# One mLSTM and SwiGLU kernel on one core: the second group's k and q as 32x32 tiles turned by VectorE, and a weight piece asked for earlier

## The chip, the cores and the metric

The kernel runs on one core of a Trainium2 chip. Times are microseconds on the device, of whole executions. A profiled execution also gives a trace: TensorE (PE), VectorE (DVE), ScalarE (ACT), GpSimd (POOL), the queue of SyncE (SP), which asks for most transfers, and the DMA engines that carry them out.

## The reference

Four batches, eight heads, 768 tokens, 40 features a head. The first half is an mLSTM cell with a running maximum in the exponents, the second half a SwiGLU block over the tokens that come out of it (d_model 320, d_ff 1536). Cut to what matters:

```python
for t in range(S):
    m_new = np.maximum(f_gate[:, :, t] + m, i_gate[:, :, t])
    f_stab = np.exp(f_gate[:, :, t] + m - m_new)
    i_stab = np.exp(i_gate[:, :, t] - m_new)
    C = f_stab * C + i_stab * outer(v_t, k_t)        # per batch and head
    n = f_stab * n + i_stab * k_t
    h_tilde = C @ q_t
    denom = np.maximum(np.abs(n @ q_t), 1.0)
    y[:, :, t] = sigmoid(o_gate_t) * h_tilde / denom
x = y as (B * S, H * D)
g = x @ w_gate
out = (g * sigmoid(g) * (x @ w_val)) @ w_out
```

The weights of the second half reach the core as 64-bit numbers and are turned into 32-bit ones there.

## The kernel before

**Groups.** The 768 tokens are six groups of 128 tokens, each for all 32 pairs of batch and head. A group passes first through the cell, then through the SwiGLU block: twelve hidden blocks (`hidden(g, m)`, m = 0 to 11, each ten matmuls into two PSUM banks, a silu on ScalarE and a product on VectorE), then the output matmuls. The cell's work on the next group is laid between the hidden blocks of this one, by hand: a dictionary `slots` says which functions run after which block, `after` does so between the output matmuls of group 0. The schedule is manual: each engine runs its instructions in the order in which the program lists them.

**The cell within a group.** Scores need k and q with features on the partitions (`kT`, `qT`), two heads in 128 rows of which each has 64, the rows past 40 being zero. The weights of the values start from running maxima: the maxima's rows go to DRAM (`M_dram`), come back spread over the partitions into `w_sb` (`weights_load`), are subtracted from the inputs on VectorE (`weights_sub`), masked on GpSimd (`weights_mask`) and raised on ScalarE (`weights_exp`).

**Two ways to turn k and q.** For group 1, `load_all` fetches k and q with tokens on partitions, and `turn(P, ...)` has PE transpose them in 64 matmuls against the identity, with copies from PSUM on ScalarE and VectorE (`turn_one`, L291 to L303). For groups 2 to 5, `load_squares` (L309) fetches 32-token by 32-feature tiles in 16 DMAs, eight of 32 features and eight of the remaining 8, into a tile whose rest is zero, and `turn_squares` (L318) turns every 32x32 block into `kT` or `qT` by two VectorE transposes of 128x1024.

**Pieces.** The SwiGLU weights come as ten pieces (`piece_load`). Pieces 0 to 6 hold the gate and value weights, in two DMAs each; the value half goes out from ScalarE's queue for pieces 0 to 4 and from SP's after that. Pieces 7 to 9 hold the output weights. A conversion of one block is a scaling of two words on ScalarE (`scale`), two bit operations on VectorE (`join`) and a sum on GpSimd or VectorE (`rounded`). Piece 2 carries blocks 2 and 3, piece 6 blocks 10 and 11. `ahead` lists which block is converted inside which hidden block: block 10's conversion is inside hidden block 7, block 11's inside 8.

**PSUM.** Hidden blocks take their two banks from a ring of four ("gen"); the cell has another ring of four ("cell").

**Homes.** `k_sb`, `q_sb`, `v_sb`, `o_sb` hold a group's inputs, `w_sb` its weights, `vw_sb` its weighted values, `x_sb` its results before they are transposed. Each serves one group after another.

**Around the change.** In the start, `sig(0)` and `sig(1)` are the sigmoids of o's two halves on ScalarE, followed there by the requests for the value halves of pieces 2 and 3. After hidden block 0 SP asks for group 1's k and q, after block 1 for piece 6, after block 2 for the maxima and v. `turn` runs after blocks 5 and 6, and the subtractions of the maxima after blocks 6 and 7.

Of the kernel before, what the change touches and what calls it, by code (L numbers as in the profile page):

```python
# [14 lines left out]
ALU = mybir.AluOpType  # L15
# [4 lines left out]
SUB = 64  # L20
# [4 lines left out]
def kernel(  # L25
# [18 lines left out]
    nc = tc.nc  # L44
# [12 lines left out]
    NKC = DM // HP  # L57
    UH = BH // 2
    UA = UH // 2
    NH = NFC + 1  # L60
# [12 lines left out]
    def flat(t):  # L73
        return t.rearrange("p c t -> p (c t)")

    def bank(name, tag="cell"):
        return psum.tile([128, 512], F32, name=name, tag=tag)

    def half(i):
        return slice(i * SUB, (i + 1) * SUB)  # L80
# [5 lines left out]
    def heads(P):  # L86
        return slice(P * UH, (P + 1) * UH)

    k_sb = const.tile([128, BH, DP], F32)
    q_sb = const.tile([128, BH, DP], F32)  # L90
    v_sb = const.tile([128, BH, D1], F32)
    o_sb = const.tile([128, BH, D], F32)
    w_sb = const.tile([128, BH, SUB], F32)
    vw_sb = const.tile([128, BH, D1], F32)
    kT = const.tile([128, PP, L], F32)
    qT = const.tile([128, PP, L], F32)
    x_sb = const.tile([128, B, DM + HP], F32)
# [4 lines left out]
    h_sb = const.tile([128, NH, TW], F32)  # L102
# [3 lines left out]
    ident = const.tile([128, 128], F32)  # L106
# [12 lines left out]
    def copy(eng, dst, src):  # L119
        if eng is nc.scalar:  # L120
            nc.scalar.copy(dst, src)
        else:
            eng.tensor_copy(dst, src)
# [16 lines left out]
    def piece_load(p, home=None):  # L140
        kind, m, n = PIECES[p]
        if kind == "gv":
            a, d = NKC, n * 128
            src = [(slice(i * HP, (i + 1) * HP), w[:, m * 128:(m + n) * 128].rearrange("(c p) f -> p c f", p=HP))
                   for i, w in enumerate((moe_w_gate, moe_w_val))]
            queues = (nc.sync, nc.scalar if p < 5 else nc.sync)
        else:
            a, d = n, DM
            src = [(slice(0, 128), moe_w_out[m * 128:(m + n) * 128].rearrange("(a p) d -> p a d", p=128))]
            queues = (nc.sync,)  # L150
        if src[0][1].dtype == F32:
            for r, w in src:
                if kind == "o":
                    nc.sync.dma_start(out=wo_sb[r, m:m + n, :], in_=w)
                else:
                    for x in range(n):
                        nc.sync.dma_start(out=wgv_sb[r, m + x], in_=w[:, :, ts(x, 128)])
            return
        if home is None:
            raw = conv.tile([128, 4 * NKC * 128], U32, name="raw")  # L160
        else:
            raw = home.rearrange("p a t -> p (a t)").bitcast(U32)
        raw = raw[:, 0:2 * a * d]
        for (r, w), queue in zip(src, queues):
            queue.dma_start(out=raw[r].rearrange("p (a d) -> p a d", a=a), in_=w.bitcast(U32))
        words = raw.rearrange("p (a d two) -> p a d two", two=2, a=a)
        raws[p] = (words[:, :, :, 0], words[:, :, :, 1])
        split(p)
# [4 lines left out]
    def split(p):  # L173
        if p in raws:
            lo, hi = raws.pop(p)
            kind, m, n = PIECES[p]
            if kind == "gv":
                for c in range(n):
                    r = slice(c * 128, (c + 1) * 128)
                    blocks[m + c] = (lo[:, :, r], hi[:, :, r], wgv_sb[:, m + c])  # L180
            else:
                for c in range(0, n, 2):
                    blocks[NFC + (m + c) // 2] = (lo[:, c:c + 2], hi[:, c:c + 2], wo_sb[:, m + c:m + c + 2, :])
# [53 lines left out]
    nc.vector.memset(k_sb[:, :, D:], 0.0)  # L237
    nc.gpsimd.memset(q_sb[:, :, D:], 0.0)
    nc.gpsimd.memset(v_sb[:, :, D:], 1.0)
    ident_b = early.tile([128, 128], BF16)  # L240
    nc.vector.tensor_copy(ident_b, ident)
    mask_b = early.tile([128, L], BF16)
# [35 lines left out]
    def late_maxima():  # L278
        nc.vector.tensor_copy(step1[:, 0:1, 0:1], f0[0:BH, end].unsqueeze(1))
        nc.vector.tensor_copy(step1[:, 1:, 0:1], f_sb[:, 0:NL - 1, last])  # L280
        nc.vector.tensor_tensor_scan(flat(M_sb), flat(step1), flat(i_sb), M0[0:BH, end], op0=ALU.add, op1=ALU.max)
# [6 lines left out]
    M_dram = tc.dram_tile([BH, S - L], F32, name="M_dram")  # L288


    def turn_one(P, src, dst, engs):  # L291
        tp = [bank("tp_kq").rearrange("p (a t) -> p a t", t=SUB) for _ in range(2)]
        for a in range(UA):
            h = P * UH + 2 * a
            for i in range(2):
                nc.tensor.transpose(tp[i][:, a, :], src[half(i), h:h + 2, :].rearrange("p h d -> p (h d)"),  # L296
                                    ident[half(i), half(i)])
        for i in range(2):
            copy(engs[i], dst[:, P * UA:(P + 1) * UA, half(i)], tp[i])

    def turn(P, eng_k, eng_q):
        turn_one(P, k_sb, kT, eng_k)
        turn_one(P, q_sb, qT, eng_q)  # L303

    SQ = 32
# [10 lines left out]
    def turn_squares(src, dst):  # L318
        for P in range(2):
            a = slice(P * UA, (P + 1) * UA)  # L320
            nc.vector.transpose(out=dst[:, a].rearrange("p a t -> p (a t)"), in_=src[:, a].rearrange("p a t d -> p (a t d)"))

    q_sq = q_sb.rearrange("p (a x) d -> p a (x d)", x=2).rearrange("p a (t d) -> p a t d", d=SQ)

    QUAD = ((0, 0), (1, 1), (0, 1), (1, 0))
# [105 lines left out]
    def seam(n, P, engs):  # L431
        engs = list(engs)
        dst = xT(n).rearrange("p c (u i s) -> p c u i s", u=B, i=2)
        for cs in (range(0, 4), range(4, NKC)):
# [6 lines left out]
            for i in range(2):  # L441
                copy(engs.pop(0), dst[:, cs[0]:cs[-1] + 1, 2 * P:2 * P + 2, i, :], tp[i])

    def weights_load(n):
        for i in range(2):
            src = M_dram[:, ds((n - 1) * L + i * SUB, SUB)].unsqueeze(0).to_broadcast([SUB, BH, SUB])
            nc.sync.dma_start(out=w_sb[half(i)], in_=src)

    def weights_sub(n, P):
        gb = g_T[:, n, heads(P)].unsqueeze(2).to_broadcast([128, UH, SUB])  # L450
        nc.vector.tensor_tensor(w_sb[:, heads(P)], gb, w_sb[:, heads(P)], op=ALU.subtract)  # L451

    def weights_mask(P):
        for i in range(2):
# [7 lines left out]
    def sig(P):  # L462
        nc.scalar.activation(o_sb[:, heads(P)], o_sb[:, heads(P)], AF.Sigmoid)
# [10 lines left out]
    A, V, G = nc.scalar, nc.vector, nc.gpsimd  # L474
# [24 lines left out]
    def first_values(P):  # L499
        nc.gpsimd.tensor_copy(w_end[:, heads(P)], W0[:, heads(P), end])  # L500
        nc.gpsimd.tensor_tensor(vw_sb[:, heads(P)], v_sb[:, heads(P)], w_end[:, heads(P)].to_broadcast([128, UH, D1]),
                                op=ALU.mult)
# [24 lines left out]
    def first_own(u):  # L527
        first_y[u] = bank("first_y", "gen")[:, 0:H * D1].rearrange("p (h d) -> p h d", d=D1)
        for h in range(H):
            nc.tensor.matmul(first_y[u][:, h, :], lhsT=W0[:, u * H + h, :], rhs=v_sb[:, u * H + h, :], start=True, stop=True)  # L530

    def first_x(u):
        y = first_y.pop(u)
        den = work.tile([128, UH, 1], F32, name="den")[:, 0:H]
        nc.vector.tensor_scalar(den, y[:, :, D:], scalar1=1.0, scalar2=None, op0=ALU.max)
        nc.vector.scalar_tensor_tensor(den, in0=y[:, :, D:], scalar=-1.0, in1=den, op0=ALU.mult, op1=ALU.max)
        nc.vector.reciprocal(den, den)
        nc.vector.tensor_tensor(x_sb[:, u, 0:DM].rearrange("p (h d) -> p h d", d=D), y[:, :, 0:D],
                                den.to_broadcast([128, H, D]), op=ALU.mult)
# [41 lines left out]
    piece_load(0)  # L581
    piece_load(1)
    late_maxima()
    first_own(1)
    first_values(1)
    first_scores(1)
    first_x(1)
    sig(0)
    sig(1)
    piece_load(2, h_sb[:, NH - NKC:])  # L590
    piece_load(3, wo_sb)
    burn(3)
    first_own(2)
# [123 lines left out]
    def load_all(dst, a, n):  # L717
        for P in range(2):
            load(dst, a, n, P)

    run = lambda f, *a: (lambda: f(*a))
# [3 lines left out]
    ahead = {m: [m + 2] for m in range(4)}  # L725
    ahead.update({4: [6], 5: [7, 8], 6: [9], 7: [10], 8: [11], 9: [], 10: [], 11: []})
    slots = {
        0: [run(first_state, 1, A), run(load_all, k_sb, k, 1), run(load_all, q_sb, q, 1)],
        1: [run(piece_load, 6, h_sb[:, NH - NKC:]), run(decay_rows)],
        2: [run(late_turns), run(weights_load, 1), run(load_all, v_sb, v, 1)],  # L730
        3: [run(decay)],
        5: [run(turn, 0, (A, A), (A, V))],
        6: [run(turn, 1, (A, A), (A, V)), run(weights_sub, 1, 0), run(weights_mask, 0), run(piece_load, 7)],
        7: [run(weights_sub, 1, 1), run(weights_mask, 1), run(nc.gpsimd.memset, q_sb, 0.0)],
        8: [run(weights_exp, 0), run(weights_exp, 1), run(weigh_values, G, 0), run(weigh_values, G, 1),
            run(piece_load, 8)],
        9: [run(do_scores), run(do_weigh, 0), run(do_weigh, 1), run(do_decayed, 2), run(load_all, o_sb, o_gate, 1)],
# [39 lines left out]
    for g in range(1, NG):  # L777
        n, f = g + 1, g + 2
# [67 lines left out]
```

## Time and profile before

| what | us |
|---|---|
| median of 3 runs | 554.64 (554.63 to 554.94) |
| profiled execution, its time | 555.16 |
| profiled execution, its span in the trace | 553.0 |
| PE busy | 546.4 (99%) |
| VectorE busy | 234.4 (42%) |
| ScalarE busy | 134.7 (24%) |
| GpSimd busy | 106.6 (19%) |

The span runs from the first to the last instruction in the trace; the profiled execution's own time is 2.2 us longer. TensorE's granted clock is full in all 40 slices of the page. Times within the trace count from the span's start.

A row of a timeline gives the start, the length, the engine (SPq is SP's queue), the line of the kernel, the operation, the tiles out<-in, and how many instructions were merged; in brackets stands how long the engine had idled and what released it. A row of a DMA list gives the transfer, the queue it was asked for from, how many, the size of each and the median time from request to landing. A row of digits is the span in 40 slices of 13.8 us, each digit the busy share in tenths.

### The profile page before, as it was taken

The numbers are of one execution on the slowest core, as the hardware profiler recorded it, in microseconds if no ns is written. First come the engines' busy times: TensorE is split into PE (matmuls) and PEld (weight loads), VectorE is DVE, ScalarE is ACT, GpSimd is POOL, SyncE is SP. The second block draws the span as 40 slices with busy tenths as digits, with TensorE's granted clock in tenths as the row PEclk, the third lists the DMA queues.
The fourth block names the chain that finished last, engine by engine and source line by source line (L and its number), as shares of the span: only waits on it lengthen the run. The fifth ranks groups of instructions, "written<-read, shape, count | busy, mean of one in ns | idle before, by whom it ended". The sixth has DMA issues, their size and how long they took to land.

```text
span 553.0 us, 11595 instructions
## 1 busy us (share of the span) xinstructions
PE 546.4 (99%) x4992; PEld 312.9 (57%) x4992; DVE 234.4 (42%) x394; ACT 134.7 (24%) x202; POOL 106.6 (19%) x97
## 2 busy tenths in 40 slices
PE   8999999999999999999999999999999999999997
PEld 4955546675545575544576455466455567444475
DVE  5956687962156332445521445531426621011100
ACT  4366564443101033110124101005110100111100
POOL 2314355574011151011133001114001200000000
PEclk9999999999999999999999999999999999999999
DMA  9999996798631763660464451395000131000000
GB/s 125 177 280 187 192 274 115 155 111 125 68 49 17 108 109 83 71 76 5 82 127 104 53 68 27 49 149 107 13 1 2 29 62 43 12 1 0 2 24 24
DMA packets 223994, 45.69 MB, mean 83 GB/s; under 512 B 214504, under 2 KB 219112, under 8 KB 223944
## 3 DMA queue, kind: packets, MB, share of 16 engines
q1 hardware_dynamic: 222036, 42.11, 46.7%
q10 hardware_dynamic: 1908, 2.85, 2.0%
q8 instruction: 39, 0.64, 0.5%
q14 instruction: 11, 0.09, 0.1%
HBM read 35.68 MB, written 4.01 MB: 72 GB/s over the span
## 4 chain that ended last, share of the span: by engine, by line
PE 92%; DMA 4%; SPq 3%; POOL 0%; DVE 0%; ACT 0%; issue 0%; ACTq 0%; POOLq 0%
PE gv_ps L648 55%; PE o_ps L664 24%; PE o_ps L671 5%; SPq L117 3%; DMA h_sb<-in_moe_w_val_dram 2%; PE inter L377 2%; PE sp L331 2%; PE intra L382 2%; DMA o_sb<-in_o_gate_dram 2%; PE add L353 1%; PE tp_kq L296 0%; POOL wgv_sb L207 0%; PE tp_x L439 0%; DVE wgv_sb L200 0%; ACT top L190 0%
## 5 line engine op out<-in xcount | busy, mean ns | idle before, releaser
L648 PE MATMUL gv_ps<-xT,wgv_sb 64*128 64x512 f32 x1440 | 317.3, 593 | 1.6 <-POOL wgv_sb L207 1.1
L648 PEld LDWEIGHTS gv_ps<-xT,wgv_sb 64*128 64x128 f32 x1440 | 139.1, 187 | 159.4 <-issue 154.6
L654 DVE TENSOR_TENSOR h_sb<-sg,gv_ps 128x512 f32<-128x512 f32 x72 | 49.5, 687 | 214.5 <-ACT sg L653 214.4
L664 PE MATMUL o_ps<-wo_sb,h_sb 128*128 128x320 f32 x480 | 130.5, 433 | 0.0
L664 PEld LDWEIGHTS o_ps<-wo_sb,h_sb 128*128 128x128 f32 x480 | 90.8, 190 | 41.0 <-issue 3.8
L653 ACT ACTIVATE sg<-gv_ps 128x512 f32<-128x512 f32 x72 | 43.0, 597 | 268.6 <-PE gv_ps L648 268.5
L362 POOL TENSOR_TENSOR C<-C,dec 128x328 f32<-128x328 f32 x20 | 14.5, 735 | 137.7 <-DVE C L369 137.6
L456 POOL TENSOR_SCALAR_AFFINE_SELECT w_sb<-w_sb 64x1024 f32<-64x1024 f32 x20 | 27.8, 1388 | 60.2 <-DVE w_sb L451 59.3
L658 ACT COPY z_sb<-o_ps 128x320 f32<-128x320 f32 x24 | 10.0, 422 | 94.7 <-PE o_ps L664 90.9
L403 POOL TENSOR_TENSOR o_sb<-o_sb,y_sb 128x640 f32<-128x640 f32 x10 | 14.3, 1428 | 79.2 <-DVE y_sb L394 79.1
L671 PE MATMUL o_ps<-wo_sb,h_sb 128*128 128x320 f32 x96 | 26.9, 437 | 0.0
L451 DVE TENSOR_TENSOR w_sb<-g_T,w_sb 128x1024 f32<-128x1024 f32 x10 | 13.2, 1355 | 27.6 <-DMA w_sb<-M_dram 27.6
L426 DVE STREAM_TRANSPOSE xT<-x_sq 128x640 f32<-128x640 f32 x16 | 12.5, 822 | 23.7 <-DMA x_sq<-x_sb 23.7
L671 PEld LDWEIGHTS o_ps<-wo_sb,h_sb 128*128 128x128 f32 x96 | 17.9, 190 | 7.2
L394 DVE TENSOR_TENSOR y_sb<-y_sb,intra 64x328 f32<-64x328 f32 x40 | 19.7, 493 | 0.8 <-PE intra L382 0.2
L369 DVE TENSOR_TENSOR C<-C,add 40x328 f32<-40x328 f32 (+1 forms) x36 | 17.7, 493 | 1.3 <-PE add L353 0.4
L207 POOL TENSOR_TENSOR wgv_sb<-wgv_sb,low 128x640 int32<-128x640 int32 x8 | 12.3, 1541 | 23.7 <-DVE wgv_sb L200 21.9
L377 PEld LDWEIGHTS inter<-C,qT 64*64 64x64 f32 x640 | 10.2, 134 | 7.3 <-issue 6.1
L341 POOL TENSOR_TENSOR vw_sb<-v_sb,w_sb 128x656 f32<-128x656 f32 x10 | 12.8, 1303 | 0.4
L338 DVE TENSOR_TENSOR w_sb<-sp,w_sb 128x512 f32<-128x512 f32 x20 | 12.7, 682 | 0.0
L460 ACT ACTIVATE w_sb<-w_sb 128x1024 f32<-128x1024 f32 x10 | 10.6, 1058 | 8.8 <-POOL w_sb L456 8.8
L397 DVE TENSOR_SCALAR den<-den 128x16 f32<-128x16 f32 x10 | 12.2, 1216 | 0.3
(129 smaller groups left out, 343.7 us busy)
## 6 DMA issues: line engine op xcount, KB each, us to landing
w_sb<-M_dram SPq DMA_DIRECT2D x10, 512.0 KB, 7.2
x_sq<-x_sb SPq DMA_DIRECT2D x128, 40.0 KB, 2.0
k_sb<-in_k_dram SPq DMA_DIRECT2D x12, 320.0 KB, 6.1
v_sb<-in_v_dram SPq DMA_DIRECT2D x12, 320.0 KB, 5.7
o_sb<-in_o_gate_dram SPq DMA_DIRECT2D x12, 320.0 KB, 5.4
raw<-in_moe_w_out_dram SPq DMA_DIRECT2D x3, 1280.0 KB, 7.8
out_dram<-z_sb SPq DMA_DIRECT2D x24, 160.0 KB, 1.8
q_sb<-in_q_dram SPq DMA_DIRECT2D x32, 64.0 KB, 2.4
```

Of the source, the lines that this page charges most:

```text
L117: nc.sync.dma_start(out=dst[:, heads(P), 0:D], in_=tokens(a, c, P))
L362: nc.gpsimd.tensor_tensor(state(s + 1)[:, a], state(s)[:, a], dec[:, s - 2, a].unsqueeze(2).to_broadcast([128, UA, D1]), op=ALU.mult)
L369: nc.vector.tensor_tensor(c, c, ps[r], op=ALU.add)
L377: nc.tensor.matmul(inter[two][half(i), a, :], lhsT=qT[half(two), P * UA + a, half(i)], rhs=state(2 * n + i)[half(two), P * UA + a, :], sta ...
L394: nc.vector.tensor_tensor(t, t, intra[i][half(c)], op=ALU.add)
L403: eng.tensor_tensor(o, o, y[:, :, 0:D], op=ALU.mult)
L456: nc.gpsimd.affine_select(w, w, compare_op=ALU.is_ge, fill=NEG, base=0, pattern=[[0, UH], [1, SUB]], channel_multiplier=-1)
L648: nc.tensor.matmul(ps[i], lhsT=wgv_sb[half(i), m, PAIRS[kc][i] if g < 2 else kc, :], rhs=x[half(i), kc, :], start=(kc == 0), stop=(kc == N ...
L653: nc.scalar.activation(sg, ps[0], AF.Silu)
L654: nc.vector.tensor_tensor(hid(g, m), sg, ps[1], op=ALU.mult)
L664: nc.tensor.matmul(p, lhsT=hid(g, m)[:, ts(u, L)], rhs=wo_sb[:, m, :], start=(m == 0), stop=(m == NFC - 1))
L671: nc.tensor.matmul(ps[u], lhsT=hid(g, m)[:, ts(u, L)], rhs=wo_sb[:, m, :], start=(m == 0), stop=(m == NFC - 1))
```

## The change

- The 64 PE transposes of group 1 and their eight PSUM copies go (`turn` and `turn_one` are deleted); `turn_squares` runs in their place, for q after hidden block 5 and for k after block 6.
- q and k of group 1 are loaded as tiles (`load_squares`), after block 0, q first. q's tiles go into `q_sb`, which GpSimd clears once more in the start; k's go into `w_sb`, which GpSimd clears at the very beginning.
- Since `w_sb` is taken, group 1's maxima come into `x_sb` (first half of the heads) and `vw_sb` (second half), in four DMAs in place of two; the subtraction reads them there and writes `w_sb`.
- `k_sb`, which the state's sums need with tokens on partitions, is still loaded as before, now after block 3.
- The clearing of `q_sb` after block 7 moves to the start.
- In the start, `piece_load(2, ...)` stands between the two sigmoids.

```diff
+    nc.gpsimd.memset(w_sb, 0.0)
...
-    def turn_one(P, src, dst, engs):
...
-    def turn(P, eng_k, eng_q):
-        turn_one(P, k_sb, kT, eng_k)
-        turn_one(P, q_sb, qT, eng_q)
...
+    k_sq1 = w_sb.rearrange("p (a x) d -> p a (x d)", x=2).rearrange("p a (t d) -> p a t d", d=SQ)
...
+    first_M = [t.rearrange("p b d -> p (b d)")[:, 0:UH * SUB].rearrange("p (h t) -> p h t", t=SUB) for t in (x_sb, vw_sb)]
+
     def weights_load(n):
         for i in range(2):
+            if n == 1:
+                for P in range(2):
+                    src = M_dram[heads(P), ds(i * SUB, SUB)].unsqueeze(0).to_broadcast([SUB, UH, SUB])
+                    nc.sync.dma_start(out=first_M[P][half(i)], in_=src)
+                continue
...
-        nc.vector.tensor_tensor(w_sb[:, heads(P)], gb, w_sb[:, heads(P)], op=ALU.subtract)
+        nc.vector.tensor_tensor(w_sb[:, heads(P)], gb, first_M[P] if n == 1 else w_sb[:, heads(P)], op=ALU.subtract)
...
     late_maxima()
+    nc.gpsimd.memset(q_sb, 0.0)
...
     sig(0)
+    piece_load(2, h_sb[:, NH - NKC:])
     sig(1)
-    piece_load(2, h_sb[:, NH - NKC:])
     piece_load(3, wo_sb)
...
-        0: [run(first_state, 1, A), run(load_all, k_sb, k, 1), run(load_all, q_sb, q, 1)],
+        0: [run(first_state, 1, A), run(load_squares, q_sq, q, 1), run(load_squares, k_sq1, k, 1)],
...
-        3: [run(decay)],
-        5: [run(turn, 0, (A, A), (A, V))],
-        6: [run(turn, 1, (A, A), (A, V)), run(weights_sub, 1, 0), run(weights_mask, 0), run(piece_load, 7)],
-        7: [run(weights_sub, 1, 1), run(weights_mask, 1), run(nc.gpsimd.memset, q_sb, 0.0)],
+        3: [run(decay), run(load_all, k_sb, k, 1)],
+        5: [run(turn_squares, q_sq, qT)],
+        6: [run(turn_squares, k_sq1, kT), run(weights_sub, 1, 0), run(weights_mask, 0), run(piece_load, 7)],
+        7: [run(weights_sub, 1, 1), run(weights_mask, 1)],
```

More of the change, by code (lines that the diff above doesn't have):

```diff
@@ L288 @@
     M_dram = tc.dram_tile([BH, S - L], F32, name="M_dram")
-    def turn_one(P, src, dst, engs):
[L292 to L299, printed above, removed]
-    def turn(P, eng_k, eng_q):
-        turn_one(P, k_sb, kT, eng_k)
-        turn_one(P, q_sb, qT, eng_q)
     SQ = 32
```

## The prediction

> **What bounds the kernel now.** I read the page's share of busy time first, then the chain of waits, then the timelines of PE, VectorE and SP's queue around the change, last the DMA issues with their time to landing.
>
> ```profile
> PE 546.4 (99%) x4992; PEld 312.9 (57%) x4992; DVE 234.4 (42%) x394; ACT 134.7 (24%) x202; POOL 106.6 (19%) x97
> DMA  9999996798631763660464451395000131000000
> ```
>
> PE is busy all the way, so work taken off PE is worth its length, if nothing else comes late. But the DMA row stands at 9 for the first six slices (83 us): in the stage that the change touches, a second resource is full, and transfers land in about the order in which SP issues them. What PE gives up there:
>
> ```profile
> 62.21 0.66 PE L296 MATMUL tp_kq<-ident,k_sb 64*128 64x64 f32 x16
> 62.70 0.67 PE L296 MATMUL tp_kq<-ident,q_sb 64*128 64x64 f32 x16
> 63.20 4.51 PE L648 MATMUL gv_ps<-xT,wgv_sb 64*128 64x512 f32 x20
> 67.55 0.66 PE L296 MATMUL tp_kq<-ident,k_sb 64*128 64x64 f32 x16
> 68.04 0.66 PE L296 MATMUL tp_kq<-ident,q_sb 64*128 64x64 f32 x16
> 68.54 13.10 PE L648 MATMUL gv_ps<-xT,wgv_sb 64*128 64x512 f32 x60
> ```
>
> The chain of waits counts each set of 32 as 0.99 us on PE. The last row is three hidden blocks (m = 7, 8, 9) of 4.37 us, so m = 9 starts at 77.3. `hidden` takes two of the four "gen" banks, so block 9 needs block 7's banks, which VectorE frees with its product at L654:
>
> ```profile
> 68.38 0.69 DVE L654 TENSOR_TENSOR h_sb<-sg,gv_ps 128x512 f32<-128x512 f32 x1 [0.83 <-ACT sg L653]
> 68.98 0.68 DVE L123 COPY qT<-tp_kq 128x512 f32<-128x512 f32 x1
> 70.97 1.22 DVE L451 TENSOR_TENSOR w_sb<-g_T,w_sb 128x1024 f32<-128x1024 f32 x1 [1.31 <-DMA w_sb<-M_dram]
> 72.12 0.49 DVE L199 TENSOR_SCALAR wgv_sb<-top 128x640 uint32<-128x640 uint32 x1
> 72.64 1.64 DVE L200 SCALAR_TENSOR_TENSOR wgv_sb<-top,wgv_sb 128x640 uint32<-128x640 uint32 x1
> 74.41 1.54 DVE L207 CUSTOM_DVE_ANT_0 wgv_sb<-wgv_sb,low 128x1280 uint16<-128x1280 uint16 x1
> 75.87 0.68 DVE L654 TENSOR_TENSOR h_sb<-sg,gv_ps 128x512 f32<-128x512 f32 x1
> ```
>
> This is the place that decides. VectorE already waits 1.31 us for the maxima (w_sb<-M_dram) and block 7's product, in order behind them, ends at 76.55: 0.7 us before PE wants its banks. How late may the maxima be? SP's queue says when they are asked for:
>
> ```profile
> 37.72 0.59 SPq L165 DMA_DIRECT2D raw<-in_moe_w_val_dram  x1
> 38.37 0.60 SPq L611 DMA_DIRECT2D M_dram<-M_sb  x1
> 39.01 11.05 SPq L117 DMA_DIRECT2D k_sb<-in_k_dram  x2
> 50.11 3.34 SPq L117 DMA_DIRECT2D q_sb<-in_q_dram  x2
> 53.54 2.31 SPq L165 DMA_DIRECT2D h_sb<-in_moe_w_gate_dram  x1
> 55.89 0.62 SPq L165 DMA_DIRECT2D h_sb<-in_moe_w_val_dram  x1
> 56.61 9.13 SPq L447 DMA_DIRECT2D w_sb<-M_dram  x2
> ```
>
> k and q stand ahead of piece 6, and that ahead of the maxima. What 32 tile loads of the same shapes (q, then k) take to issue is seen later, where DMA is at 0.66 of its share and nothing is ahead of them:
>
> ```profile
> 132.19 8.42 SPq L315 DMA_DIRECT2D q_sb<-in_q_dram  x16
> 140.71 10.04 SPq L315 DMA_DIRECT2D k_sq<-in_k_dram  x16
> ```
>
> 18.5 us for 32, 0.577 each. Times to landing, of the windows that hold one such DMA each:
>
> ```profile
> raw<-in_moe_w_val_dram SPq DMA_DIRECT2D x1, 640.0 KB, 12.5
> h_sb<-in_moe_w_val_dram SPq DMA_DIRECT2D x1, 640.0 KB, 10.4
> q_sb<-in_q_dram SPq DMA_DIRECT2D x1, 320.0 KB, 8.9
> ```
>
> So piece 5's value half lands at 37.72 + 12.5 = 50.2, the second q load (issued 51.42) at 60.3, piece 6's value half at 55.89 + 10.4 = 66.3, and the maxima are there at 70.97, 4.7 later.
>
> [...] L321 takes 1.22 us for 128x1024. [...] The old loads have runs of 160 B, 2048 in each; the tiles have 128 B and 32 B, 512 in each. The page of before counts 214504 of 223994 packets under 512 B, which fits. [...] L200 takes 0.83 us alone and 1.64 at 72.64, beside GpSimd's mask.
>
> **The change part by part.**
> 1. Off PE: the 64 transposes, 2 x 0.99 = 2.0 us, on the path.
> 2. Off ScalarE: six copies from PSUM (some 3.3 us). ScalarE idles 1.9 us before each silu here: nothing.
> 3. On VectorE: four transposes, 4 x 1.22 = 4.9, less two copies of 0.68: +3.5 us between 64 and 72. It idles 2.4 us there (0.30 before block 9's conversion, 0.83 and 1.31 in the rows above), so even with no late DMA block 7's product would end 1.1 later, at 77.6; PE, now 2.0 ahead, would wait for it and start block 9 at 77.6, not 77.3: +0.3 in place of -2.0.
> 4. Piece 2's value half goes out from ScalarE's queue after the first sigmoid (ends 22.3), not after the second (25.4, which waits for o). It landed at 39.0 and held block 2 (PE idle 1.08 us before 43.1). From 3 us earlier and up it comes well inside the first blocks: -1.1 us on PE. It also lets two queues run earlier; I take 1.2 us off piece 5's landing: 49.0 (bounds: 0 and 2.7, the single queue's worst and best overlap).
> 5. SP's queue, between M_dram's store and v 38 DMAs where there were 8: q's 2 and k's 2 become 16 each, before piece 6; the maxima's 2 become 4; k_sb's own 2 now come after v. The compiled order shows eight completion semaphores used in turn: each DMA waits for the one eight before it. Tiles 2 to 7 wait for pieces 2 to 5, the seventh for piece 5's value half. So six are out when it lands at 49.0, and 26 remain: 26 x 0.577 = 15.0 (bounds: the median instruction, 0.487, 12.7; 0.65 as in the contended stretch at 82.65, 16.9). Piece 6 is asked for at 64.0, not 53.5.
> 6. The last tile lands 2.5 later (its group's median), 66.5 where q's last was 60.3. Piece 6 took 6.0 from there, the maxima 4.7: 72.5 and 77.2. The first subtraction needs three quarters of the maxima, 1.2 less: 76.0, against 70.97.
> 7. GpSimd: a 1.80 us memset of w_sb near 2.6, where it idles 8.9 us; q_sb's moves from 80.8 to 19.7, ahead of values read at 36. The maxima's first homes (x_sb, last read by PE near 30; vw_sb, by `first_state` at 37.5) are free when asked for. k_sb is needed by the state sums after block 10 and lands near 86. All at nothing; their cover is that slack.
>
> Sum at block 9: VectorE restarts at 76.0 where it did at 70.97, +5.0. Its next 5.6 us have the same instructions, so block 7's product ends at 81.6, not 76.55; PE starts block 9 at 81.6, not 77.3: **+4.3 us**. PE's gains of parts 1 and 4 lie before this wait and are swallowed. Block 8's product follows 5.5 us later, 87.1, before block 10 is due (87.9 after scores). What is late next: pieces 7 and 8, near 90 and 93, wanted by block 10's conversions near 89: 0 to 1. I take 0.3: **+4.6**. Behind it PE is full as before and only shifted. Piece 9 lands near 110 and is wanted at 112.
>
> The profiled execution has a span of 553.0 and a time of 555.16, 0.5 above the median 554.64. So 559.8 against its own time, **559.2** as a median.
>
> **The rivals.**
> - A, likeliest: tile loads delay piece 6 and the maxima, VectorE waits, PE after it. With part 5's and 4's bounds: (-2.3 -1.5 to +1.9 +1.2) around 4.6, +0.8 to +7.7. Against it: nothing in the trace runs 32 tiles in a full queue; they might go at their minimum, 0.33.
> - B, the other side: transfers do not decide. If the remaining tiles took under 0.38 each (26 x 0.2 = 5 us less), VectorE would find the maxima when its transposes end. Then its own work is the bound (part 3's +0.3), all of it begun 1.1 earlier by part 4: -0.8, or 553.8; with VectorE's work hidden too, the whole -3.1, or 551.5. For it: some tile issues are that short. Against: the mean of 32 undisturbed ones is 0.577, and the queue must also wait for landings.
> - C: a second late transfer behind A. Piece 9 waits for 16 more tiles and o's landings; 3 us over part 6's sum make it later than its conversion at 112, and the copies of the next inputs stand behind that on ScalarE. +8 to +11: 563 to 566.
> - D: the change doesn't do what it says: the tiles land in time, but the sigmoids' order moves nothing, since the transfers share one set of engines anyway. Part 3's +0.3 alone: 554.9.
>
> **How the numbers follow.** A 0.77, C 0.10, B 0.09, D 0.04. A change of 0.2% (1.1 us) is about what a measurement of this kernel can tell from none. A gives slower but for its lowest end; B splits between faster and same. Faster 0.07, same 0.07, slower 0.86. Range 555.0 to 563.8: A's bounds, cut to what leaves B's faster part below and most of C above.
>
> **What would show it.** Right: SP issues piece 6 near 64 after 32 tile loads; VectorE idles some 5 us at the first subtraction, put down to the maxima's DMA; PE shows a gap of 6 to 8 us before block 9 and none before block 2; after 90 us both traces run alike, shifted. Wrong: no gap before block 9; tiles issued in under 10 us; or VectorE waiting at the tile transposes, which would move the cause from the maxima to k.

## The result, and the profile after

| what | before | after |
|---|---|---|
| median, us (4 runs each) | 554.79 (554.63 to 557.83) | 563.62 (563.44 to 563.87) |
| profiled execution, span, us | 553.0 | 561.6 |
| PE busy, us | 546.4 | 550.1 |
| mean granted TensorE clock | 1.00 | 0.988 |

The ratio is 1.0143 [1.0119, 1.0167]: 8.8 us slower. The forecast was 559.2 with a range of 555.0 to 563.8. The side and the place were right; the size lay 0.2 us inside the far edge. The page after (engines' busy time, then the clock and the DMA share in 40 slices of 14.04 us, then packets):

```profile
PE 550.1 (98%) x4928; PEld 315.4 (56%) x4928; DVE 239.4 (43%) x396; ACT 131.9 (23%) x196; POOL 108.9 (19%) x98
...
PEclk9989988999999999999999999999999999999999
DMA  9998799698642395353295253195000131000000
...
DMA packets 236795, 46.36 MB, mean 83 GB/s; under 512 B 227304, under 2 KB 231912, under 8 KB 236744
```

PE has 64 instructions fewer and is busy 3.7 us longer, which can't be more work: the clock row has 8s in the third slice (28 to 42 us) and in the sixth and seventh (70 to 98 us), where before it was full everywhere. There are 12801 packets more than before's 223994. The DMA row falls to 8 and 7 in slices 4 and 5 (42 to 70 us), where before it stood at 9: while SP asks for the tiles, the engines that carry them are less busy than before, not more.

SP's queue after, the rows that the prediction named (start, length, tiles, number merged):

```profile
39.68 0.60 SPq L608 DMA_DIRECT2D M_dram<-M_sb  x1
40.33 16.41 SPq L302 DMA_DIRECT2D q_sb<-in_q_dram  x16
56.79 8.45 SPq L302 DMA_DIRECT2D w_sb<-in_k_dram  x16
65.33 0.60 SPq L165 DMA_DIRECT2D h_sb<-in_moe_w_gate_dram  x1
```

Piece 6 is asked for at 65.33, not 53.54. The 32 tile loads take 24.9 us of the queue. The second half of them takes 8.45, the price that the undisturbed ones had; the first half takes twice that, because it waits for pieces that are still arriving: single tiles go out at 44.38, 47.64 and 50.14, each some 0.1 us or less behind the landing of a half of piece 4 or 5 (44.37, 47.53 and 50.06). The last of these, with piece 5's value half, asked for at 39.02, as the DMA list has it:

```profile
50.14 1.29 SPq L302 DMA_DIRECT2D q_sb<-in_q_dram  x1
raw<-in_moe_w_val_dram SPq DMA_DIRECT2D x1, 640.0 KB, 11.0
```

From 50.14 on 27 tiles follow in 15.2 us, 0.56 each. VectorE's timeline shows what is late:

```profile
72.54 2.37 DVE L308 STREAM_TRANSPOSE kT<-w_sb 128x1024 f32<-128x1024 f32 x2
78.57 1.23 DVE L447 TENSOR_TENSOR w_sb<-g_T,x_sb 128x1024 f32<-128x1024 f32 x1 [3.67 <-DMA x_sb<-M_dram]
79.71 0.48 DVE L199 TENSOR_SCALAR wgv_sb<-top 128x640 uint32<-128x640 uint32 x1
80.23 1.64 DVE L200 SCALAR_TENSOR_TENSOR wgv_sb<-top,wgv_sb 128x640 uint32<-128x640 uint32 x1
82.01 1.54 DVE L207 CUSTOM_DVE_ANT_0 wgv_sb<-wgv_sb,low 128x1280 uint16<-128x1280 uint16 x1
83.47 0.68 DVE L651 TENSOR_TENSOR h_sb<-sg,gv_ps 128x512 f32<-128x512 f32 x1
```

The same chain as before, begun at 78.57 instead of 70.97: the two transposes take 2.37, then VectorE waits 3.67 for the maxima. k's tiles are not what it waits for. Block 7's product ends at 84.15, not 76.55: 7.6 us later. PE's timeline, and block 10 as it was before:

```profile
56.80 22.58 PE L645 MATMUL gv_ps<-xT,wgv_sb 64*128 64x512 f32 x102
84.20 6.46 PE L645 MATMUL gv_ps<-xT,wgv_sb 64*128 64x512 f32 x18 [4.82 <-DVE h_sb L651]
90.59 2.10 PE L319 MATMUL sp<-qT,kT 64*64 64x64 f32 x128
92.62 4.56 PE L645 MATMUL gv_ps<-xT,wgv_sb 64*128 64x512 f32 x20
...
83.59 4.56 PE L648 MATMUL gv_ps<-xT,wgv_sb 64*128 64x512 f32 x20
```

The first two of block 9's twenty matmul instructions (two for each of the ten matmuls) are still in the row of 102; the other 18 wait 4.82 us for block 7's product and then take 6.46 where 18 of 4.37 / 20 take 3.9. The windows say why (columns: busy time and number for PE, weight loads, VectorE, ScalarE, GpSimd; then the granted clock, the DMA share and GB/s):

```profile
80.00:84.00 4.00, 0.00 (x0) 0.00 (x0) 3.83 (x4) 2.02 (x4) 2.81 (x2) 0.66 1.50 162
84.00:88.00 4.00, 3.80 (x10) 1.75 (x12) 3.83 (x5) 2.28 (x2) 2.60 (x2) 0.50 1.41 169
```

After the gap PE works at half clock (0.50 from 84 to 88 us). Block 10 starts at 92.62 instead of 83.59 (the last row), 9.0 later: 6.5 until the 18 go on (84.20 against 77.7, block 9's start of 77.3 and two matmuls) and 2.5 of half clock. From there no idle time of PE over 0.15 us is left; the span ends 8.6 later.

A second place differs, which the prediction had at nothing. The timeline of the start, after, in order of time: GpSimd's clearing of `w_sb` and VectorE's cast beside it, GpSimd's subtraction, VectorE's copy and GpSimd's clearing of `q_sb`, then PE (`burn` is matmuls on constant data that keep PE busy) and the clock; last, the same copy, matmuls and block 0 before:

```profile
2.50 1.80 POOL L240 MEMSET w_sb<- 128x2048 f32 x1
...
2.94 1.44 DVE L242 CAST ident_b<-ident 128x128 bf16<-128x128 f32 x1
...
18.75 1.53 POOL L277 TENSOR_TENSOR i_sb<-i_sb,f_sb 32x640 f32<-32x640 f32 x1
...
19.81 2.25 DVE L281 COPY keep<-f_sb 32x9 f32<-32x9 f32 x1
...
20.24 1.79 POOL L580 MEMSET q_sb<- 128x2048 f32 x1
...
24.33 0.81 PE L465 MATMUL burn<-junk 128*128 128x512 bf16 x3 [1.52 <-DVE h_sb L519]
24.97 5.36 PE L526 MATMUL first_y<-v_sb,h_sb 128*128 128x41 f32 x32
...
24.00:36.00 12.00, 11.67 (x83) 10.08 (x83) 8.75 (x25) 3.62 (x6) 1.56 (x3) 0.72 1.05 286
...
19.29 0.43 DVE L280 COPY keep<-f_sb 32x9 f32<-32x9 f32 x1
...
22.88 3.66 PE L530 MATMUL first_y<-v_sb,h_sb 128*128 128x41 f32 x32
...
31.90 4.56 PE L648 MATMUL gv_ps<-xT,wgv_sb 64*128 64x512 f32 x20 [0.53 <-DVE m_in L285]
```

The copy of nine columns, 0.43 before, took 2.25 and ended with the clearing (22.06 and 22.03); the cast, 0.15 before, took 1.44 and ended with the other one (4.38 and 4.30). The copy began 0.43 before the clearing, while GpSimd's subtraction was running (18.75 to 20.28), and lasted until both were done. PE then idles 1.52, and `first_y` takes 5.36 where it took 3.66: from 24 to 36 us the mean clock is 0.72. Block 0 starts at 36.77, not 31.90. Whether these 4.9 us reach the end is what the experiments had to tell.

### The profile page after: what moved, and what is told of

Read it like the earlier page. It is cut to its first block, busy times and chain, and to the rows that moved or that the text cites. A ratio compares the mean times of both kernels' runs of the same rounds, so it can differ in the third digit from the quotient of the medians.

```text
span 561.6 us, 11513 instructions
## 1 busy us (share of the span) xinstructions
PE 550.1 (98%) x4928; PEld 315.4 (56%) x4928; DVE 239.4 (43%) x396; ACT 131.9 (23%) x196; POOL 108.9 (19%) x98
## 4 chain that ended last, share of the span: by engine, by line
PE 94%; DVE 2%; DMA 2%; ACT 1%; issue 1%; SPq 0%; ACTq 0%; DVEq 0%
PE gv_ps L645 53%; PE o_ps L661 23%; PE o_ps L668 5%; PE inter L365 2%; DMA x_sb<-M_dram 2%; PE sp L319 2%; PE intra L370 2%; PE first_y L526 2%; PE add L341 1%; PE tp_x L557 1%; PE tp_kq L505 1%; PE sp L515 1%; PE wps L476 0%; PE burn L465 0%; ACT low L192 0%
## 5 line engine op out<-in xcount | busy, mean ns | idle before, releaser
L645 PEld LDWEIGHTS gv_ps<-xT,wgv_sb 64*128 64x128 f32 x1440 | 140.9, 188 | 164.8 <-issue 153.0
L447 DVE TENSOR_TENSOR w_sb<-g_T,w_sb 128x1024 f32<-128x1024 f32 x8 | 10.8, 1390 | 26.7 <-DMA w_sb<-M_dram 26.7
L385 DVE TENSOR_SCALAR den<-den 128x16 f32<-128x16 f32 x10 | 12.2, 1215 | 0.3
```

The lines of the kernel that those rows point to most:

```text
L645: nc.tensor.matmul(ps[i], lhsT=wgv_sb[half(i), m, PAIRS[kc][i] if g < 2 else kc, :], rhs=x[half(i), kc, :], start=(kc == 0), stop=(kc == N ...
```

## The experiments

Two theories were set against each other. **T**: the tile loads delay the maxima, and the gap on PE costs its length and the half clock behind it; what happens in the start is swallowed by that wait. **R**: the start's delay (the clearings, piece 2) adds to the end. Before's medians beside the three series (1 to 4, 5 to 8, 9 to 12) were 554.99, 554.95 and 554.90.

**1. Piece 2 alone**, in the kernel before:

```diff
     sig(0)
+    piece_load(2, h_sb[:, NH - NKC:])
     sig(1)
-    piece_load(2, h_sb[:, NH - NKC:])
```

> The kernel before with one edit: piece 2 asked for between the two sigmoids. Theory T (the tile loads delay the maxima, the rest of the change is a small gain): piece 2 lands some 3 us or more earlier, PE's wait of 1.08 us before hidden block 2 goes, 1.0 to 1.1 us faster, 553.6. Rival (the transfers share one set of engines, so an earlier request moves nothing, or delays pieces 0 and 1): within 0.3 us of before, or slower by up to 0.5.

557.22 median of 22 runs, 21 of them from 553.04 to 560.81; ratio 1.0016 [0.9997, 1.0035]. The gain of 1.1 us did not come: block 2 finds its piece, but block 0 starts at 33.29, 1.4 late. In the profiled run, itself near the median, piece 5's value half is asked for at 41.27 (before 37.72): the early request did not let the queues run earlier, it went with a later start. How much of that start is the request's doing is open: the clock is half for some 3.4 us from 26 us on, though PE is never idle there (the last section comes back to this, experiments 9 to 12 to the request).

**2. One clearing alone**, in the kernel before:

```diff
     late_maxima()
+    nc.gpsimd.memset(q_sb, 0.0)
     first_own(1)
```

> The kernel before with one addition: GpSimd clears q_sb in the start, where the changed kernel does. In the changed kernel the VectorE copy beside that clearing took 2.25 us in place of 0.43, PE idled 1.5 us and ran at a granted clock of 0.65 for 10 us, and hidden block 0 began 4.9 us late (36.77 for 31.90). If the clearing does that (T and rival R alike): block 0 begins 3 to 5 us late here, and since no late maxima swallow it, 3 to 4 us slower, 558 to 559. If it is something else in the changed kernel (the earlier clearing of w_sb, the transfers): under 1 us slower.

558.52 median of 20 runs, ratio 1.0041 [1.0023, 1.006]. The times fall into two heaps: seven from 553.9 to 557.1 with a mean clock of 0.999 or 1.0, thirteen from 557.9 to 559.8 with 0.994 or less. The profiled run is of the second heap:

```profile
19.34 1.96 DVE L280 COPY keep<-f_sb 32x9 f32<-32x9 f32 x1
...
23.57 0.81 PE L469 MATMUL burn<-junk 128*128 128x512 bf16 x2 [1.24 <-DVE h_sb L523]
24.21 5.81 PE L530 MATMUL first_y<-v_sb,h_sb 128*128 128x41 f32 x32
```

The copy alone, 1.5 us longer (1.96 for 0.43) and at its end with the clearing again (21.30 and 21.27), makes PE idle 1.24, and in such a run block 0 starts at 36.28, 4.4 later. So a clearing is not free in a kernel whose block 9 waits for nothing: 3.5 us at the median, 2.3 by the ratio. The heap without the slow clock lies less than 1 us above before, so most of it goes with the clock.

**3. After, with both clearings moved** behind block 1's conversion:

```diff
-    nc.gpsimd.memset(w_sb, 0.0)
...
-    nc.gpsimd.memset(q_sb, 0.0)
...
     convert(1)
+    nc.gpsimd.memset(q_sb, 0.0)
+    nc.gpsimd.memset(w_sb, 0.0)
```

> The changed kernel with both clearings by GpSimd moved to after block 1's conversion (near 36 us), where VectorE is idle. T: block 0 begins on time, near 32, but block 9 still waits for the maxima, which come only as much earlier as pieces 4 and 5 are asked for earlier, 1.3 us; so 1 to 2 us faster than the changed kernel, 561.6 to 562.6, with a gap before block 9 near 8 us for 4.8. Rival R (the late start is a loss of its own, added to the wait): the whole 4.9 us come back, 558.7.

565.39 (561.68 to 565.45, 4 runs), ratio 1.0158 [1.013, 1.0187]; not faster than after. The idle time at 24 us is gone (beside the clearings' new place, 38.41 to 41.95, VectorE's L199 takes 2.59 at 39.70, where before it took 0.49 at 40.01), but block 0 still starts at 34.55, because piece 0's scaling now waits for its own transfer. ScalarE's timeline:

```profile
31.18 0.77 ACT L190 ACTIVATE top<-raw 128x640 f32<-128x640 f32 x1 [3.03 <-DMA raw<-in_moe_w_gate_dram]
```

Before, it began at 28.50 after 0.39 of waiting. Block 0 is 2.2 us earlier than in after and the end is not. That does not yet refute R: behind the wait block 0 runs at half clock (6.26 us for 4.56), and block 1, at 41.80, is only 0.5 earlier than in after (42.32). T's own gain missed too. What decides shows in SP's queue: piece 5's value half goes out at 42.18 (39.02 in after), and piece 6 at 65.36 as in after (65.33).

**4. After, with PE kept busy** through the gap, by 18 matmuls on junk after block 8:

```diff
-        8: [run(weights_exp, 0), run(weights_exp, 1), ...
+        8: [run(burn, 18), run(weights_exp, 0), run(weights_exp, 1), ...
```

> The changed kernel with 18 matmuls on constant data between hidden blocks 8 and 9, which fill PE's wait of 4.8 us and feed nothing. In the changed kernel the granted clock is 0.50 from 82 to 88 us and block 9's last 18 rows take 6.46 us for 3.95. If the idle gap takes the clock down (T): the clock stays at 1.0, block 9 takes its 3.95 us again, 2.0 to 2.5 us faster than the changed kernel, 561.1 to 561.6. If the slow block has another cause (operands late, banks): no change or slower by what the filler overruns, 563.6 to 564.

566.97 (564.14 to 569.0, 4 runs), ratio 1.0202 [1.0166, 1.0237]. Locally it did what it was to show, PE:

```profile
77.87 4.06 PE L465 MATMUL burn<-junk 128*128 128x512 bf16 x17
81.86 1.12 PE L645 MATMUL gv_ps<-xT,wgv_sb 64*128 64x512 f32 x2
84.80 4.56 PE L645 MATMUL gv_ps<-xT,wgv_sb 64*128 64x512 f32 x18 [1.82 <-DVE h_sb L651]
...
142.79 13.53 PE L645 MATMUL gv_ps<-xT,wgv_sb 64*128 64x512 f32 x60 [3.18 <-ACT z_sb L655]
```

The 18 matmuls begin 0.6 later than in after and take 4.56, not 6.46; the clock in 80 to 88 us is 1.00. Block 10 is 1.3 earlier, at 91.31. So the half clock is caused by the gap. Then more than the gain is lost: at 142.79 PE waits 3.18 for `z_sb`. ScalarE there waits 7.80 for group 0's output store, which SP issues at 137.86 (135.44 in after), behind the next group's loads. In after ScalarE has that wait too, 3.85 long, and PE doesn't feel it. Why SP runs later here was not isolated.

**5. The tiles alone**: after without the other two parts (piece 2 back behind both sigmoids, clearings as in experiment 3).

```diff
     sig(0)
-    piece_load(2, h_sb[:, NH - NKC:])
     sig(1)
+    piece_load(2, h_sb[:, NH - NKC:])
```

> The changed kernel with piece 2 back behind both sigmoids and both clearings moved to after block 1's conversion: only the tiles and the maxima's homes are left. T: pieces 0 and 1 come on time again, block 0 starts near 32 us as before the change, but 26 of the 32 tiles still go out after piece 5 lands, piece 6 is asked for at 64 to 66, the first subtraction starts at 77 to 79 and block 9 at 83 to 85, so 8 to 10 us slower than before, 562.5 to 564.5, with a gap before block 9 of 8 to 9 us. R (start and wait are losses that add up): 4 to 5 us slower, 558.7 to 560.

562.40 (561.52 to 563.37, 4 runs), ratio 1.0131 [1.0096, 1.0167]. SP, VectorE and PE:

```profile
63.48 0.60 SPq L165 DMA_DIRECT2D h_sb<-in_moe_w_gate_dram  x1
...
77.00 1.23 DVE L446 TENSOR_TENSOR w_sb<-g_T,x_sb 128x1024 f32<-128x1024 f32 x1 [4.96 <-DMA x_sb<-M_dram]
...
82.63 7.18 PE L645 MATMUL gv_ps<-xT,wgv_sb 64*128 64x512 f32 x18 [5.82 <-DVE h_sb L651]
```

Block 0 starts at 33.35, 3.4 earlier than in after; piece 6 is asked for 1.85 earlier, and the span ends 1.0 earlier. Most of the loss is the tiles.

**6. q's tiles only**: as 5, but k is loaded whole and turned by PE again, and the maxima go to `w_sb`.

```diff
-        0: [run(first_state, 1, A), run(load_squares, q_sq, q, 1), run(load_squares, k_sq1, k, 1)],
+        0: [run(first_state, 1, A), run(load_squares, q_sq, q, 1), run(load_all, k_sb, k, 1)],
...
-        5: [run(turn_squares, q_sq, qT)],
-        6: [run(turn_squares, k_sq1, kT), ...
+        5: [run(turn_squares, q_sq, qT), run(turn_one, 0, k_sb, kT, (A, A))],
+        6: [run(turn_one, 1, k_sb, kT, (A, A)), ...
```

> As the kernel with the tiles alone, but only q comes as tiles; k is loaded whole and turned by TensorE, and the maxima go to w_sb as before the change. 16 tiles less stand ahead of piece 6 and 2 whole loads more. T: piece 6 is asked for near 59 us, the first subtraction starts 4 to 5 us later than before the change (75 to 76), block 9 follows near 81, 4 to 6 us slower than before, 558.5 to 561: about half of the loss with all 32. If not the tiles in the queue but VectorE's own transposes or the homes of the maxima cost: within 1 us of before.

559.72 (559.0 to 560.3, 5 runs), ratio 1.0081 [1.0054, 1.0108]. Piece 6 is asked for at 55.93, and

```profile
73.64 1.23 DVE L448 TENSOR_TENSOR w_sb<-g_T,w_sb 128x1024 f32<-128x1024 f32 x1 [5.70 <-DMA w_sb<-M_dram]
...
79.27 6.25 PE L646 MATMUL gv_ps<-xT,wgv_sb 64*128 64x512 f32 x18 [3.48 <-DVE h_sb L652]
```

Half of the added transfers gives 2.7 of experiment 5's 6.0 us at the subtraction, and 4.8 of its 7.45 us at the end. The share at the end is larger, since of the half clock's price the smaller gap still pays 2.3 us, the larger 3.3 (6.25 and 7.18 for the 18, against 3.9).

**7. k's tiles behind piece 6 and the maxima**, in `wo_sb` while that is free, turned after block 7 (the maxima go to `w_sb` again; otherwise as 5):

```diff
-        0: [run(first_state, 1, A), run(load_squares, q_sq, q, 1), run(load_squares, k_sq1, k, 1)],
+        0: [run(first_state, 1, A), run(load_squares, q_sq, q, 1)],
...
-        2: [run(late_turns), run(weights_load, 1), run(load_all, v_sb, v, 1)],
+        2: [run(late_turns), run(weights_load, 1)],
-        3: [run(decay), run(load_all, k_sb, k, 1)],
+        3: [run(decay), run(nc.gpsimd.memset, k_sq1, 0.0), run(load_squares, k_sq1, k, 1), run(load_all, v_sb, v, 1), run(load_all, k_sb, k, 1)],
...
-        6: [run(turn_squares, k_sq1, kT), run(weights_sub, 1, 0), ...
-        7: [run(weights_sub, 1, 1), run(weights_mask, 1)],
+        6: [run(weights_sub, 1, 0), ...
+        7: [run(turn_squares, k_sq1, kT), run(weights_sub, 1, 1), run(weights_mask, 1)],
```

> As the kernel with the tiles alone, but k's 16 tiles are asked for behind piece 6 and the maxima (into wo_sb, free by then, cleared after block 3) and turned after block 7; the maxima go to w_sb as before the change. The same instructions on every engine, another order in SP's queue. T: piece 6 is asked for near 56 us, the first subtraction starts at 71.5 to 73.5, the wait before block 9 falls to 2 to 4 us, and some comes back before block 10, since k's transposes now stand ahead of block 8's product: 1 to 4 us slower than before, 556 to 559, 5 us or more faster than with k's tiles in front. R or a cost of VectorE's transposes: as with the tiles in front, 562 to 564.

564.14 (561.14 to 565.27, 4 runs), ratio 1.0154 [1.011, 1.0198]. T's forecast missed. The maxima are on time and block 9 has no gap, but VectorE, then PE, wait elsewhere:

```profile
69.70 1.22 DVE L439 TENSOR_TENSOR w_sb<-g_T,w_sb 128x1024 f32<-128x1024 f32 x1
...
77.33 2.37 DVE L307 STREAM_TRANSPOSE kT<-wo_sb 128x1024 f32<-128x1024 f32 x2 [2.05 <-DMA wo_sb<-in_k_dram]
...
85.21 6.25 PE L637 MATMUL gv_ps<-xT,wgv_sb 64*128 64x512 f32 x18 [2.16 <-DVE h_sb L643]
...
139.17 15.23 PE L637 MATMUL gv_ps<-xT,wgv_sb 64*128 64x512 f32 x60 [3.41 <-ACT z_sb L647]
```

The wait has moved from the maxima to k's tiles, one block later, again with a half clock behind it; at 139 us there is the wait of experiment 4 once more. In both orders what stands last in the queue is late; the order chose who waits.

**8. No tiles, but as many transfers**: the kernel before, with group 1's k and q asked for twice, the second time into `o_sb` and `v_sb`, which are loaded with their own contents afterwards.

```diff
-        0: [run(first_state, 1, A), run(load_all, k_sb, k, 1), run(load_all, q_sb, q, 1)],
+        0: [run(first_state, 1, A), run(load_all, k_sb, k, 1), run(load_all, q_sb, q, 1), run(load_all, o_sb, k, 1), run(load_all, v_sb, q, 1)],
```

> The kernel before with q and k of group 1 asked for twice, the second time into o_sb and v_sb, which are free then and are loaded anew later. No tile, no VectorE transpose, no clearing is added, only 4 transfers of 320 KB [...] ahead of piece 6. T: [...] the first subtraction at 78 to 79, and block 9 waits 6 to 7 us: 7 to 10 us slower than before, 562 to 565. If what costs is particular to tiles or to VectorE: under 2 us slower.

565.74 (564.46 to 566.02, 4 runs), ratio 1.0184 [1.0142, 1.0225].

```profile
81.18 1.22 DVE L451 TENSOR_TENSOR w_sb<-g_T,w_sb 128x1024 f32<-128x1024 f32 x1 [9.31 <-DMA w_sb<-M_dram]
...
86.81 6.00 PE L648 MATMUL gv_ps<-xT,wgv_sb 64*128 64x512 f32 x18 [6.41 <-DVE h_sb L654]
```

PE's transposes and all copies are still there, and no VectorE transpose, no new home, no clearing and no moved piece 2: the stall is the same kind, and larger (the start is later too: block 0 at 34.00, since piece 0 landed late). Only eight DMAs stand ahead of piece 6 here, against 32 tile loads. Put beside each other, by the runs of bytes ahead of piece 6 (2048 in a whole load, 512 in a tile load; the page after has 12800 packets under 512 B more than before's, for 12288 runs more: the tiles' 16384 less q's 4096), and the queue's time from M_dram's store to piece 6:

| kernel | runs ahead | DMAs ahead | queue time, us | first subtraction |
|---|---|---|---|---|
| before | 8192 | 4 | 15.2 | 70.97 |
| q tiles only (6) | 12288 | 18 | 18.1 | 73.64 |
| tiles alone (5) | 16384 | 32 | 24.7 | 77.00 |
| after | 16384 | 32 | 25.7 | 78.57 |
| whole loads twice (8) | 16384 | 8 | 23.3 | 81.18 |

The queue's time goes with the runs, not with the DMAs: 8 and 32 of them take 23.3 and 24.7. Nor with the bytes: the tiles carry the same 1280 KB as the loads before, experiment 8 twice that. In each kernel 10 to 12 us of the time is the wait for piece 5's value half; behind its landing the rest goes out at some 900 to 1250 runs a us.

**9 and 10. The value halves of pieces 2 and 3 earlier and later**, in the kernel before, without tiles. What stayed open was whether the early piece 2 makes piece 0 late (**Q**: ScalarE's queue takes bandwidth from what SP's asked for first) or piece 0's landing varies by itself (**V**).

```diff
# 9
+    piece_load(2, h_sb[:, NH - NKC:])
+    piece_load(3, wo_sb)
     sig(0)
     sig(1)
-    piece_load(2, h_sb[:, NH - NKC:])
-    piece_load(3, wo_sb)
```

```diff
# 10
-    piece_load(2, h_sb[:, NH - NKC:])
-    piece_load(3, wo_sb)
...
     scale(0)
+    piece_load(2, h_sb[:, NH - NKC:])
+    piece_load(3, wo_sb)
```

> The kernel before, with the value halves of pieces 2 and 3 asked for ahead of both sigmoids (some 3 to 6 us earlier on ScalarE's queue). Theory Q: transfers asked for on ScalarE's queue take bandwidth from pieces 0 and 1, which SP's queue asked for before; then piece 0's scaling waits 2 us or more for its own transfer and starts at 30.5 or later (28.50 in the kernel before), block 0 starts at 34 or later, and the median is 555 to 559. Rival V: piece 0's landing varies from run to run whatever ScalarE's queue does; then the scaling starts at 28 to 29.5 here too, block 2 finds its piece, and the median is 553.5 to 555.

> The kernel before, with the value halves of pieces 2 and 3 asked for behind the scaling of piece 0 (some 4 us later on ScalarE's queue), the opposite dose. Q: piece 0's scaling waits for no transfer and starts at 28.0 to 28.3, when ScalarE's copies end; the price is paid by block 2, which waits 3 to 5 us for piece 2 (1.08 in the kernel before), so 556 to 559 with the half clock behind that wait. V: piece 0's scaling starts where it did, with a wait or without one, and block 2 waits the same 3 to 5 us.

Earlier: 556.73 (20 runs), ratio 1.0022 [1.0006, 1.0037]. Piece 0's scaling starts at 29.34 and waits for no transfer; block 0 starts at 33.90 all the same, 2.0 late (some 1.2 of it behind a half clock near 28 us, without idle time; see the last section), and block 2 finds its piece. Later: 556.40 (20 runs), ratio 1.0026 [1.0015, 1.0037]. The scaling starts at 28.00 without a wait, and block 2 waits 2.27 (1.08 before). The place before had is better than either; Q is not confirmed, since the strongest dose shows no wait for piece 0.

**11 and 12. The tiles with piece 2 late and early, side by side**: experiment 5's kernel once more, and experiment 3's.

```diff
     sig(0)
+    piece_load(2, h_sb[:, NH - NKC:])
     sig(1)
-    piece_load(2, h_sb[:, NH - NKC:])
```

> The change's tiles alone once more, piece 2 behind both sigmoids and both clearings moved behind block 1's conversion, on the same chip as the next run. Q and V: piece 0's scaling starts at 28 to 29.5; 561.5 to 563.5 again, with the first subtraction near 77.

> The same with piece 2's value half between the sigmoids, the only difference. Q: piece 0's scaling waits 1.5 to 3 us and starts near 31, block 0 at 34.5, piece 6 is asked for 1 to 2 us later than in the tiles alone, and the median is 1 to 3 us above it. V: the two starts differ by less than 1 us and the medians by less than 1 us.

562.05 (561.36 to 562.58) and 563.86 (561.47 to 566.38), 4 runs each; ratios to before 1.0126 [1.0111, 1.0141] and 1.0145 [1.011, 1.018]. The intervals overlap, and the second kernel's runs lie two low and two high; the profiled one is the highest. In it ScalarE waits 3.68 for o's second half and then

```profile
31.72 0.77 ACT L190 ACTIVATE top<-raw 128x640 f32<-128x640 f32 x1 [3.07 <-DMA raw<-in_moe_w_gate_dram]
```

where the kernel with piece 2 late started at 28.09 without a wait. Piece 0's gate half landed 11.7, 11.9 and 12.2 us after its request in experiments 3, 4 and 12, which have the tiles and the early piece 2. But after has both as well, and there it took 9.3; experiments 1 and 9, with the early request, have 8.8 and 8.6, and experiment 8, without it, 11.5. So the early request alone doesn't make piece 0 late. What sorts most profiles is whether SP was still issuing piece 0 when ScalarE asked for piece 2. In 3, 4 and 12 it was (requests at 21.00, 20.85 and 22.51, SP's issue done at 21.99, 21.94 and 23.12); in after and 9 it had just finished (20.97 and 20.84, done at 20.27 and 20.58). Experiment 1 lies between (22.03, done at 22.62), and experiment 8 needs another reason. No run isolates this, so the cause stays open.

What the pair does show is how a late start reaches the end. Block 0 starts at 31.84 and 35.09, piece 5's value half is asked for at 37.79 and 42.18, piece 6 at 63.12 and 66.39, the first subtraction is at 76.48 and 79.92. SP's queue hands the delay on: the 32 tiles follow M_dram's store, that follows piece 5, and piece 5 waits for its home in the start. In after, block 0 was 4.9 later than in experiment 11, piece 6 only 2.2, and the span ended 1.8 later. Experiment 12 and after have the same delay at block 1 (42.34 and 42.32 against 37.40), but block 10 is 3.3 and 1.6 late, near the delay of their piece 6, 3.3 and 2.2. So neither theory stands as put: the start's delay is neither swallowed nor added whole; what reaches block 10 is the part that SP's queue takes over. (Experiment 12's span ends 4.8 later than 11's; 0.8 of the rest is a wait for `z_sb` at 143 us.)

None of these kernels is shown to beat the one before.

## Why the prediction was right, by its own steps

- **Part 1, the 64 transposes off PE (-2.0).** They are gone (4928 instructions for 4992), and the gain does not appear at the end, since it lies before the wait, as the sum had it.
- **Part 3, four VectorE transposes.** Priced at 1.22 each, 2.37 a pair measured.
- **Part 4, piece 2 (-1.1, and piece 5 1.2 earlier).** Wrong: piece 2's wait is gone (after has none before block 2), but alone it is no gain (experiment 1). Piece 5's value half was asked for at 39.02, later than before, not earlier, and landed at 50.06 (50.26 before): the 1.2 us did not come. Together with the clearings it cost 1.0 and 1.8 us in the span (after against experiments 5 and 11).
- **Part 5, the tiles in SP's queue (piece 6 at 64.0).** 65.33 measured, 63.48 and 63.12 with the tiles alone. Right: 27 tiles at 0.56 behind piece 5's landing, for 26 at 0.577, and the 1.3 us more is nearly all that landing, 50.06 for 49.0. What the picture lacked is why a tile has this price. It counted DMAs; experiment 8 has eight of them in place of experiment 5's 32 with nearly the same time (23.3 us for 24.7) and as many runs (16384), so what fills the queue is the number of runs.
- **Part 6, the landing (first subtraction at 76.0).** 78.57 measured. 1.3 of the 2.6 is piece 6's later request (part 5). The other 1.2 is a term that was too small: from piece 6's request to the first subtraction I took 12.0, and it was 13.2 (13.5 and 13.4 in experiments 5 and 11).
- **Part 7, the clearings at nothing.** Wrong. The cover named was GpSimd's own idle time; what I did not ask was what VectorE does beside it. The one pair that I had looked at was L200 beside GpSimd's mask (1.64, and 0.83 alone); VectorE's copies and casts I left out, and one copy took 2.25 for 0.43. Alone a clearing costs 3.5 us at the median, 2.3 by the ratio (experiment 2). What it costs in after was not isolated: experiment 3, with the clearings moved, has a late piece 0 instead. By experiments 11 and 12 what counts up to block 10 is the part that delays piece 6.
- **The sum at block 9 (+4.3).** The product was 7.6 late, not 5.0; its slack to PE was 1.15, not 0.7, so the 18 matmuls are 6.5 late. And a term is missing: **the half clock behind the gap, 2.5 us**. The forecast foretold a gap of 6 to 8 us and costed it at its length alone; 4.8 came, as PE itself ran late from the start. Behind the gap of 4.82 the clock stands at 0.50 from 84 to 88 us; experiment 4, with most of the gap filled, has 1.00 there. The nine longest gaps in these traces, 3.41 to 6.41 us (one each in after and experiments 3, 5, 6, 7, 8, 11, two in 12), all have a half clock in them or behind them. In after the clock had fallen 1.9 us into the gap (the column before the last two):

```profile
79.40:81.20 1.80, 0.00 (x0) 0.00 (x0) 1.76 (x3) 0.00 (x0) 1.33 (x1) 1.00 1.45 178
81.30:84.20 2.90, 0.00 (x0) 0.00 (x1) 2.76 (x4) 2.21 (x4) 1.58 (x1) 0.50 1.52 156
```

Of shorter gaps some brought it (2.16 in experiment 7) and others not (2.27 in experiment 10, 1.82 and 3.18 in experiment 4).
- **Next in line.** Pieces 7 and 8 and piece 9 were not late; rival C did not come in after. Its kind of wait did come in experiments 4 and 7, in another place: the output stores in SP's queue.

So 559.2 against 563.6: at block 10, 4.3 + 2.2 (block 9's wait, 6.5 against 4.3) + 2.5 (the clock) are 9.0, of which 8.6 remain in the span; the 0.3 kept for what is late next did not come. That the range held 563.6 is luck: rival A, which came true, was put at +7.7 at most, short of the measured 8.8, and the range reached further only for rival C, which did not come in after.

## What to carry to other kernels

Before transfers are cut finer, count the runs of bytes that the finer form puts ahead of what the bounding engine waits for next: here 2.0 us of PE work were saved for 8192 runs more, and the end came 8.8 us later. When a change makes TensorE wait, add the half clock behind the gap to the gap's length: here it came with each of the nine longest gaps (3.41 to 6.41 us), for 1.7 to 3.3 us more, and with some shorter ones (one of 2.16); when it puts a GpSimd instruction into idle time, look at what VectorE runs beside it first. A saving or delay that lies before a longer wait counts only as far as it moves the request that ends that wait.

## What the runs showed that was not expected

- A GpSimd clearing of 1.80 us, which reads nothing, stretched VectorE's small copies and casts from 0.43 to 2.25 and from 0.15 to 1.44.
- In the start the clock fell by no rule that PE's idle time gives. Behind an idle time of 1.24 and 1.52 us (experiment 2, after) it was half for some 7 us; behind 1.29 in experiment 4 it stayed full. In experiments 1, 5, 7 and 9 it was half for some 3.4 us with PE busy all the time; experiment 9's window, with PE's busy time in the third place and the clock third from the end:

```profile
26.00:32.00 6.00, 6.00 (x36) 4.57 (x36) 5.13 (x15) 3.12 (x6) 0.78 (x2) 0.72 1.09 278
```

Block 0 starts at 33.3 to 33.9 in these four, and near 31.9 in before and experiments 6, 10 and 11, whose clock stays full there. Experiments 5 and 11 are one kernel, so it varies from execution to execution. What takes the clock down in that stretch of small matmuls is open.
- With piece 2 asked for 3 to 4.5 us earlier on ScalarE's queue, piece 0's gate half, which SP's queue had asked for before, landed some 3 us later in three profiles (31.09, 31.01 and 31.63 in experiments 3, 4 and 12, against 28.42 before), and not in after and experiments 1 and 9 (27.98, 28.33 and 27.84).
